# Sending the last 2 MB zero fill of GpSimd's queue as four transfers of 56, 1, 64 and 7 rows

## The chip, the cores and the metric

One core of one Trainium2 chip. The metric is device time in microseconds (us), the median over executions of the whole program. The kernel before takes 800.08 us (three runs, 799.72 to 800.21); nearly all executions here agree within 0.3%, so a few us can be told apart when runs share a chip. There are exceptions: four executions of the kernel before, on two of the chips, took 802.4 to 803.1 us, so gains of 2 to 3 us are read from several runs and with their interval.

Engines in the profile: PE is TensorE, DVE VectorE, ACT ScalarE, POOL GpSimd, SP SyncE. Transfers are issued from SyncE, ScalarE and GpSimd, and share the core's sixteen DMA engines: in the queue view below two queues fill 64.0% and 34.8% of the sixteen engines' time.

## The reference, cut to what matters

A one-token decode step (attention over the last 4,096 rows of a 32,768-row cache, then a gated layer) and its gradients for all inputs. What matters here is the size of two of the outputs: the gradients of the two caches, each 8 x 32,768 x 256 in bf16. Only the last 4,096 rows of each head carry values. The other 28,672 rows are zero, and the kernel has to write them:

```python
k = jnp.repeat(k_cache[:, :, Sk - W:, :], rep, axis=1)   # W = 4096 of Sk = 32768 rows
v = jnp.repeat(v_cache[:, :, Sk - W:, :], rep, axis=1)
...
_out, _vjp = jax.vjp(_f, A_x, A_k_cache, A_v_cache, A_wq, A_wo, B_w_gate, B_w_up, B_w_down)
_grads = _vjp(grad_out)          # d k_cache and d v_cache are zero outside the window
```

## The kernel before: the parts that matter

Nearly all of the on-chip memory (SBUF, 128 partitions side by side) is one tile, `arena`, cut by hand into column ranges. A framework (the tile layer) sees every instruction's reads and writes of a tile, orders the instructions and puts in the semaphore waits. The zero source, `zeros`, is the first ZW = 8,192 columns of that tile, of which `ar(off, n)` is the n columns from off.

```python
    TOTAL = RB + 50 * KB                          # 99,328 columns of bf16
    arena = const.tile([128, TOTAL], bf16)

    def ar(off, n):
        return arena[:, off:off + n]
    ...
    zeros = ar(0, ZW)                             # ZW = 8192: columns 0 to 8191
    ...
    s_off = RB + 38 * KB + 9 * D
    dgb = ar(s_off, 1280)
    diag = ar(s_off + 1280, 640)                  # columns 98,496 to 99,135
```

GpSimd issues 103 fills of 2 MB (128 rows of 16 KB), each reading `zeros` (13 of them its first half twice). The first 55 go out one after another in the first 344 us. The second half of `zeros` is then lent to the weight blocks, is zeroed again after the second of three blocks, and the remaining fills follow.

```python
    def send_fills(n0, n1, halves=False):
        for reg in fills[n0:n1]:
            if halves:
                ...
            else:
                ZQ.dma_start(out=reg, in_=zeros)              # line 132; ZQ is GpSimd
    ...
        for n in range(len(BLOCKS)):                          # three weight blocks
            ...
            for i in range(2):
                nc.vector.tensor_tensor(out=diag[:, 0:w]..., in0=ident_f..., in1=dgu_f...)   # line 410
                for m in range(2):
                    nc.tensor.matmul(bc_ps..., lhsT=ones_bf[:], rhs=diag...)                 # line 414
                    nc.scalar.copy(out=dgb..., in_=bc_ps...)                                 # line 415
            ...
            if n == 1:
                nc.vector.memset(ar(ZW // 2, ZW // 2), 0.0)   # line 426
                send_fills(HALF1, len(fills))
```

Nearly all of the backward pass hangs on the third block's lines 410 to 421. The last fills of all are issued from SyncE at the end, behind the results:

```python
        for o, g, n0, n1, f in late_jobs:
            reg = zero_rows(o, g, n0, n1, f)
            for i in range(reg.shape[0]):
                LD.dma_start(out=reg[i], in_=ar(2 * ZW - f, f))   # LD is SyncE
```

Of the kernel before, what the change touches and what calls it, by code (L numbers as in the profile page):

```python
# [26 lines left out]
ZW = 8192  # L27
HALF0, HALF1 = 42, 55
# [5 lines left out]
def kernel(  # L34
# [4 lines left out]
    ZQ = nc.gpsimd  # L39
# [13 lines left out]
    def ar(off, n):  # L53
        return arena[:, off:off + n]
# [4 lines left out]
    zeros = ar(0, ZW)  # L59
# [54 lines left out]
    def zero_rows(o, g, n0, n1, f):  # L114
        reg = o[0, g, 0:Sk - W, :].rearrange("s d -> (s d)")[n0 * 128 * ZW:n1 * 128 * ZW]
        return reg.rearrange("(n p f) -> n p f", p=128, f=f)

    late_jobs = [(out_2, G - 1, 5, 7, 2 * ZW), (out_3, G - 1, 0, 6, 2 * ZW), (out_3, G - 1, 6, 7, ZW)]
    fills = []
    for g in range(G):  # L120
        for o in (out_2, out_3):
            if g == G - 1 and o is out_3:
                continue
            reg = zero_rows(o, g, 0, 5 if g == G - 1 else NZ, ZW)
            fills += [reg[i] for i in range(reg.shape[0])]
# [4 lines that stand above are left out]
                ZQ.dma_start(out=reg.rearrange("p (k f) -> p k f", k=2), in_=zeros[:, 0:ZW // 2].unsqueeze(1).to_broadcast([128, 2, ZW // 2]))  # L130
            else:
                ZQ.dma_start(out=reg, in_=zeros)  # L132
# [206 lines left out]
    def block_views(n):  # L339
        f0, nb = BLOCKS[n]  # L340
        w = 128 * nb
        wgu = ar(wgu_off[n % 2], 8 * w).rearrange("p (c i f) -> p c i f", c=4, i=2)
        wd = ar(wd_off[n % 2], nb * D).rearrange("p (b n) -> p b n", n=D)
        return f0, nb, w, wgu, wd

    def load_block(n):
        f0, nb, w, wgu, wd = block_views(n)
        for eng, i, wt in ((LD, 0, B_w_gate), (nc.scalar, 1, B_w_up)):
            eng.dma_start(out=wgu[:, 0:3, i, :], in_=wt[0:384, :].rearrange("(c p) f -> p c f", c=3)[:, :, f0:f0 + w])
            eng.dma_start(out=wgu[0:DQ, 3, i, :], in_=wt[384:D, f0:f0 + w])  # L350
        LD.dma_start(out=wd, in_=B_w_down[f0:f0 + w, :].rearrange("(p b) n -> p b n", b=nb))
# [4 lines left out]
    with tc.tile_pool(name="ps_mid", bufs=3, space=bass.MemoryType.PSUM) as ps_mid, \  # L356
# [34 lines left out]
        for n in range(len(BLOCKS)):  # L391
            f0, nb, w, wgu, wd = block_views(n)
            b0 = f0 // 128
            cs = slice(b0, b0 + nb)
            for b in range(nb):
                nc.vector.tensor_tensor_reduce(out=dgb[:, 0:D], in0=wd[:, b, :], in1=dh2_bc[:], scale=1.0, scalar=0.0,
                                               op0=ALU.mult, op1=ALU.add, accum_out=d_hh[:, b0 + b:b0 + b + 1])
            gu_ps = ps_mid.tile([128, 2, 5], f32, tag="mid", name="gu_ps")
            for i in range(2):
                for b in range(nb):  # L400
                    for k in range(4):
                        kp = DQ if k == 3 else 128
                        nc.tensor.matmul(gu_ps[:, i, b:b + 1], lhsT=wgu[0:kp, k, i, b::nb], rhs=X2_b[0:kp, k:k + 1], start=(k == 0), stop=(k == 3))
            nc.vector.tensor_copy(out=gu_f[:, :, cs], in_=gu_ps[:, :, 0:nb])
            for i in range(2):
                nc.vector.tensor_tensor(out=dgu_f[:, i, cs], in0=d_hh[:, cs], in1=gu_f[:, 1 - i, cs], op=ALU.mult)
            nc.vector.tensor_tensor(out=hh_f[:, cs], in0=gu_f[:, 0, cs], in1=gu_f[:, 1, cs], op=ALU.mult)
            nc.vector.tensor_copy(out=hh_bf[:, cs], in_=hh_f[:, cs])
            for i in range(2):
                nc.vector.tensor_tensor(out=diag[:, 0:w].rearrange("p (m b) -> p m b", b=nb), in0=ident_f[:].unsqueeze(2).to_broadcast([128, 128, nb]),  # L410
                                        in1=dgu_f[:, i, cs].unsqueeze(1).to_broadcast([128, 128, nb]), op=ALU.mult)
                for m in range(2):
                    bc_ps = ps_mid.tile([128, 320], f32, tag="mid", name="bc_ps")
                    nc.tensor.matmul(bc_ps[:, 0:w // 2], lhsT=ones_bf[:], rhs=diag[:, m * w // 2:(m + 1) * w // 2], start=True, stop=True)
                    nc.scalar.copy(out=dgb[:, w * i + m * w // 2:w * i + (m + 1) * w // 2], in_=bc_ps[:, 0:w // 2])
            for b in range(nb):
                nc.tensor.matmul(ffn_ps[:], lhsT=hh_bf[:, b0 + b:b0 + b + 1], rhs=wd[:, b, :], start=(b0 + b == 0), stop=(b0 + b == NF - 1))
            for c in range(4):
                kp = DQ if c == 3 else 128
                wc = wgu[0:kp, c].rearrange("p i f -> p (i f)")  # L420
                nc.vector.tensor_tensor_reduce(out=wc, in0=wc, in1=dgb[0:kp, 0:2 * w], scale=1.0, scalar=0.0,  # L421
                                               op0=ALU.mult, op1=ALU.add, accum_out=dhn[0:kp, c, n:n + 1])
            if n + 2 < len(BLOCKS):
                load_block(n + 2)
            if n == 1:
                nc.vector.memset(ar(ZW // 2, ZW // 2), 0.0)
                send_fills(HALF1, len(fills))

        dcat2 = workm.tile([128, 8], f32)
        nc.vector.reduce_sum(out=dcat2[:, 0:4], in_=dhn[:], axis=AX)  # L430
# [57 lines left out]
    with tc.tile_pool(name="work2", bufs=2) as work2, tc.tile_pool(name="lnw", bufs=1) as lnw, \  # L488
# [164 lines left out]
        for o, g, n0, n1, f in late_jobs:  # L653
            reg = zero_rows(o, g, n0, n1, f)
# [31 lines left out]
```

## Time and profile before

| | before |
|---|---|
| median time | 800.08 us |
| span of the profiled run | 798.4 us |
| bytes moved | 334.8 MB |
| VectorE busy / TensorE busy | 51% / 59% |

The slice view of the kernel before cuts the span into 40 equal slices; a digit is a busy share in tenths, and the last row is the rate of all transfers.

```profile
DVE  2116584765846783143791579467574139573000
...
DMA  9999999999999999999999999999999999999996
GB/s 351 429 432 429 430 430 429 429 429 427 429 422 425 426 419 417 413 423 424 422 423 408 430 429 429 432 424 428 423 429 420 426 424 427 419 424 426 427 436 261
```

The DMA row is full almost everywhere: this kernel is bound by its transfers. The queue part of the page (packets, MB, share of the sixteen engines' time) shows whose they are: q0 is GpSimd's queue, q1 SyncE's.

```profile
q0 software_dynamic: 16496, 216.01, 64.0%
q1 hardware_dynamic: 11382, 116.68, 34.8%
```

The windows view of the last 16 us (busy time of each engine, then granted TensorE clock, DMA share and GB/s):

```profile
core 0: us, PE busy (x) PEld busy (x) DVE busy (x) ACT busy (x) POOL busy (x), PEclk, DMA share, GB/s
782.00:788.00 6.00, 0.00 (x0) 0.00 (x0) 0.00 (x0) 0.00 (x0) 0.00 (x0) 0.50 0.96 410
788.00:792.00 4.00, 0.00 (x0) 0.00 (x0) 0.00 (x0) 0.00 (x0) 0.00 (x0) 0.50 0.60 258
792.00:796.00 4.00, 0.00 (x0) 0.00 (x0) 0.00 (x0) 0.00 (x0) 0.00 (x0) 0.50 0.08 33
796.00:798.40 2.40, 0.00 (x0) 0.00 (x0) 0.00 (x0) 0.00 (x0) 0.00 (x0) 0.50 0.02 7
```

All engines of the core are idle and the share falls slowly: 0.08 over 4 us is little more than one DMA engine of sixteen. The trace keeps a completion record for each DMA engine of a transfer (without the engine's number). For the last store they read 789.0 us (first), 791.4 (median), 793.8 (second last) and 797.2 (last).

### The profile page before, as it was taken

How to read it: one execution, taken by the hardware profiler on the slowest of the kernel's cores; microseconds unless marked ns; L12 is line 12 of the kernel's file. 1: busy time of each engine (PE TensorE's matmuls, PEld its weight loads, DVE VectorE, ACT ScalarE, POOL GpSimd, SP SyncE). 2: the span in 40 equal slices, each digit the busy share in tenths (PEclk: the TensorE clock that was granted, in tenths of full speed). 3: DMA queues.
4: the chain of work that ended last, by engine and by line, in shares of the span. 5: the costliest groups of instructions: out<-in, count | busy, mean ns of one | idle time of the engine just before them, and what ended most of it. 6: DMA issues, size and time to landing. Idle time of an engine off the chain costs nothing.

```text
span 798.4 us, 7905 instructions
## 1 busy us (share of the span) xinstructions
PE 469.3 (59%) x3159; PEld 242.1 (30%) x3182; DVE 408.4 (51%) x728; ACT 196.2 (25%) x309; POOL 61.4 (8%) x112
## 2 busy tenths in 40 slices
PE   0459999999999998532319568565236027261000
PEld 0334545545445444311207434332103012020000
DVE  2116584765846783143791579467574139573000
ACT  0142314124132201000101127463333016242000
POOL 4000000010101111100210001000000000000000
PEclk9989999999999999555557869785558558565555
DMA  9999999999999999999999999999999999999996
GB/s 351 429 432 429 430 430 429 429 429 427 429 422 425 426 419 417 413 423 424 422 423 408 430 429 429 432 424 428 423 429 420 426 424 427 419 424 426 427 436 261
DMA packets 29354, 334.80 MB, mean 419 GB/s; under 512 B 2819, under 2 KB 5894, under 8 KB 7814
## 3 DMA queue, kind: packets, MB, share of 16 engines
q0 software_dynamic: 16496, 216.01, 64.0%
q1 hardware_dynamic: 11382, 116.68, 34.8%
q10 hardware_dynamic: 1440, 1.61, 0.6%
q8 instruction: 25, 0.41, 0.2%
q14 instruction: 11, 0.09, 0.0%
HBM read 53.69 MB, written 280.59 MB: 419 GB/s over the span
## 4 chain that ended last, share of the span: by engine, by line
PE 40%; DMA 28%; DVE 15%; ACT 4%; issue 2%; another core or an unknown queue 0%; SPq 0%; ACTq 0%; DVEq 0%
DMA out_dram<-arena 18%; PE M_ps L309 13%; PE ok_ps L313 8%; PE rows_ps L255 7%; PE tr_ps L252 5%; DMA dh_bc<-in_grad_out_dram 4%; ACT arena L269 3%; DVE arena L643 2%; DVE arena L644 2%; DMA arena<-in_A_wo_dram 2%; DVE arena L452 2%; PE dqb_ps L495 2%; DMA arena<-in_B_w_up_dram 2%; DMA arena<-in_B_w_gate_dram 2%; DVE arena L421 2%
## 5 line engine op out<-in xcount | busy, mean ns | idle before, releaser
L304 DVE TENSOR_TENSOR arena<-arena,p_f 128x2048 bf16<-128x2048 bf16 x64 | 145.2, 2284 | 58.7 <-PE M_ps L309 58.7
L309 PE MATMUL M_ps<-arena 128*128 128x512 bf16 x489 | 126.4, 381 | 1.1
L255 PE MATMUL rows_ps<-arena,vpad 128*16 128x512 bf16 x256 | 85.6, 430 | 23.1 <-DVE arena L606 17.1
L252 PE MATMUL tr_ps<-ident_bf,arena 128*128 128x128 bf16 x1024 | 87.8, 236 | 14.2 <-DMA arena<-in_A_k_cache_dram 7.2
L132 POOL DMA_DIRECT2D out_dram<-arena x90 | 48.2, 537 | 549.4 <-DMA out_dram<-arena 495.6
L252 PEld LDWEIGHTS <-arena 128*128 128x128 bf16 x1024 | 66.0, 105 | 63.5 <-issue 55.6
L636 PE MATMUL d_ps<-arena,rT 32*128 32x512 bf16 x256 | 44.6, 508 | 67.1 <-DVE arena L644 49.1
L269 ACT COPY arena<-tr_ps 128x1024 bf16<-128x1024 bf16 x64 | 61.7, 1015 | 69.3 <-PE tr_ps L252 69.3
L313 PE MATMUL ok_ps<-arena 128*16 128x256 bf16 x512 | 64.6, 273 | 1.1 <-DVE arena L296 0.9
L309 PEld LDWEIGHTS <-arena 128*128 128x128 bf16 x512 | 43.3, 99 | 51.0 <-issue 15.3
L604 ACT COPY arena<-tr_ps 128x1024 bf16<-128x1024 bf16 x32 | 32.5, 1017 | 95.7 <-PE tr_ps L252 39.1
L640 ACT CAST arena<-d_ps 128x512 bf16<-128x512 f32 x64 | 37.7, 589 | 72.4 <-PE d_ps L636 72.4
L643 DVE CAST arena<-d_ps 128x512 bf16<-128x512 f32 x64 | 43.9, 686 | 14.2 <-PE d_ps L636 14.0
L313 PEld LDWEIGHTS <-arena 128*16 128x16 bf16 x512 | 41.9, 89 | 29.9 <-issue 21.0
L644 DVE CAST arena<-d_ps 128x512 bf16<-128x512 f32 x64 | 43.5, 679 | 7.6 <-DMA out_dram<-arena 7.6
L636 PEld LDWEIGHTS <-rT 32*128 32x128 bf16 x256 | 11.5, 95 | 93.9 <-issue 51.1
L641 ACT CAST arena<-d_ps 128x512 bf16<-128x512 f32 x64 | 38.1, 595 | 7.5 <-DMA out_dram<-arena 7.5
L255 PEld LDWEIGHTS <-vpad 128*16 128x16 bf16 x256 | 19.3, 91 | 57.0 <-issue 49.3
L507 DVE CUSTOM_DVE_ANT_0 arena<-arena 128x4096 bf16<-128x4096 bf16 x3 | 13.1, 4422 | 24.4 <-ACT arena L500 24.4
L284 ACT ACTIVATE e_f<-cols_ps,nbias 128x32 f32<-128x32 f32 x16 | 4.5, 286 | 85.7 <-DVE nbias L280 85.7
L257 DVE COPY arena<-rows_ps 16x512 f32<-16x512 f32 x16 | 10.8, 675 | 28.7 <-PE rows_ps L255 28.7
L606 DVE COPY arena<-tr_ps 128x1024 bf16<-128x1024 bf16 x32 | 21.7, 680 | 3.5 <-PE tr_ps L252 3.4
(198 smaller groups left out, 373.8 us busy)
## 6 DMA issues: line engine op xcount, KB each, us to landing
out_dram<-arena POOLq DMA_DIRECT2D x103, 2048.0 KB, 52.6
out_dram<-arena SPq DMA_DIRECT2D x18, 2048.0 KB, 33.8
arena<-in_A_v_cache_dram SPq DMA_DIRECT2D x10, 2048.0 KB, 49.4
arena<-in_A_k_cache_dram SPq DMA_DIRECT2D x8, 2048.0 KB, 28.6
out_dram<-arena SPq DMA_DIRECT2D x4, 4096.0 KB, 46.1
arena<-in_A_wq_dram SPq DMA_DIRECT2D x2, 3072.0 KB, 20.4
arena<-in_A_wo_dram SPq DMA_DIRECT2D x2, 1792.0 KB, 16.2
out_dram<-arena SPq DMA_DIRECT2D x2, 1792.0 KB, 32.9
```

The costliest lines, as they stand in the source:

```text
L132: ZQ.dma_start(out=reg, in_=zeros)
L252: nc.tensor.transpose(tr_ps[:, dh, i, :], X_sb[:, 4 * q + i, dh * 128:(dh + 1) * 128], ident_bf[:])
L255: nc.tensor.matmul(rows_ps[:], lhsT=pad[:, dh, 16 * q:16 * q + 16], rhs=XT[:, dh].rearrange("p t k -> p (t k)"), start=(q == 0 and dh == 0 ...
L269: sT_ps = dots(kv_at(K_off[g]), KT_slot, vpad[g % 2], rows1, ps_c, "cols", lambda q, XT, ps: nc.scalar.copy(out=XT, in_=ps))
L304: nc.vector.tensor_tensor(out=pK, in0=K_sb[:, 4 * c:4 * c + 4, :].unsqueeze(2).to_broadcast([128, 4, 2, Dh]), in1=p_f[:, c::8, :].unsqueez ...
L309: nc.tensor.matmul(M_ps[:, vh, :], lhsT=V_sb[:, t, vh * 128:(vh + 1) * 128], rhs=pK[:, i, :, :].rearrange("p h d -> p (h d)"), start=(t == ...
L313: nc.tensor.matmul(ok_ps[:, k, :], lhsT=ppad[g % 2][:, 8 * (t % 4) + t // 4, :], rhs=X_sb[:, t, :], start=(g == 0 and k == 0 and t == 0), ...
L636: nc.tensor.matmul(d_ps[:, qi].rearrange("p w d -> p (w d)"), lhsT=rT[32 * q:32 * (q + 1), :], rhs=RB_[32 * q:32 * (q + 1), l, :], start=T ...
L640: nc.scalar.copy(out=stV[:, t:t + 2, :], in_=d_ps[:, :, 0, :])
L641: nc.scalar.copy(out=stK[:, t:t + 2, :], in_=d_ps[:, :, 1, :])
L643: nc.vector.tensor_copy(out=stV[:, t:t + 2, :], in_=d_ps[:, :, 0, :])
L644: nc.vector.tensor_copy(out=stK[:, t:t + 2, :], in_=d_ps[:, :, 1, :])
```

## The change

Intent: one DMA engine of sixteen ends the kernel alone. By a premise of the prediction (its source is given there), a transfer from GpSimd whose outermost size is k below sixteen goes on k engines. So the last fill is cut in such a way that one engine (number 7, if the count starts at 0) gets one row, its seven other rows going to engines 0 to 6. To keep every engine reading from its own place in SBUF, the source rows are taken from every fourth partition, and each is read repeatedly.

```diff
             if n == 1:
                 nc.vector.memset(ar(ZW // 2, ZW // 2), 0.0)
-                send_fills(HALF1, len(fills))
+                send_fills(HALF1, len(fills) - 1)
+                reg = fills[-1]
+                for p0, step, r0, k, m in ((0, 4, 0, 7, 8), (28, 4, 127, 1, 1), (64, 4, 56, 8, 8), (0, 4, 120, 7, 1)):
+                    ZQ.dma_start(out=reg[r0:r0 + k * m].rearrange("(k m) f -> k m f", m=m),
+                                 in_=zeros[p0:p0 + step * (k - 1) + 1:step].unsqueeze(1).to_broadcast([k, m, ZW]))
```

## The prediction

> **What bounds the kernel now.** Transfers. In the slice view the DMA row is at nine tenths in 39 of 40 slices; the DMA part gives 334.8 MB at a mean of 419 GB/s over 798.4 us. PE is busy 59%, DVE 51%, and the timeline shows no compute after 734 us. The change writes the same 2 MB, so only the balance of the sixteen DMA engines can move.
>
> That balance is not perfect. In the windows view the DMA share is 0.97 in 780 to 788 us, 0.77 in 788 to 790, 0.44, then 0.10 in 792 to 794 and 0.06 in 794 to 796 (25 GB/s): one engine of sixteen works alone at the end. The completion records of the last store agree: its engines report at 789.0 (first), 791.4 (median), 793.8 (second last) and 797.2 us (last). GpSimd's last fill: 731.1 first, 736.8 second last, 741.5 last; on most earlier fills the last report is 2 to 10 us behind the second. It looks like one fixed slow engine. The Trainium skill, "DMA: Bandwidth & Descriptors", section "Latency and other measured facts", says that engines 7 and 15 are usually slower; the trace carries no engine number, so it cannot say which.
>
> **What the change does.** The same page, section "Why a DMA increments its semaphore by 16 and not by 1", says that a GpSimd transfer whose outermost size is k below 16 goes on k consecutive engines from a round-robin cursor. If the cursor stands at 0, the 56 rows are engines 0 to 6 with eight rows each, the single row is engine 7, the 64 rows are engines 8 to 15 with eight each, and the last seven rows go to 0 to 6. Engine 7 does one row instead of eight, engines 0 to 6 nine.
>
> **Cost.** In the tail, a store of eight 16 KB rows per engine takes about 4.9 us (spacing of successive stores' reports), so a row is 0.62 us. Seven rows off: 4.3 us. If engine 7 is the straggler, it ends at 797.2 - 4.3 = 792.9; engines 0 to 6 end 0.6 later than now; the second-slowest then ends last, at 793.8 (794.4 if it is one of 0 to 6). Gain 2.8 to 3.4 us, all on the critical path, since the stream on that engine is unbroken to the end.
>
> Added: three more GpSimd issues of about 0.53 us (timeline of POOL). Each waits for the landing of an earlier fill: I expect issues at about 688, 692, 702 and 712 us, ahead of 725 to 731 us, where their bytes come up. That costs nothing.
>
> **Prediction.** 797.0 us, range 796.2 to 800.6; chances: faster by over 2% 0.01, within 2% 0.98, slower by over 2% 0.01. About 65% for a gain of some 3 us, 20% for none (the slow engine is another), 15% for a cursor elsewhere (0 to 0.6 us slower, or more if shares pile up on a few engines).
>
> **What would show it.** Right: the last store's second-last and last reports under 1.5 us apart, a steeper fall of the DMA share at the end, same bytes, issues at the times above. Wrong: the straggler still alone for 3 us and a span of 798 or 799. If the clusters pile up on the same engines, half of the engines end some 5 us early.
>
> **What would make it wrong.** The cursor does not start at 0, or keeps its place between executions (it advances by 23, so by 7 modulo 16), which would spread repeated runs; the straggler is another engine; or a transfer with k below 16 is spread differently.

## More of the kernel before

GpSimd's fills are filler for stretches in which SyncE has nothing ready.

VectorE at the third block's line 410 (the timeline: start, duration, instruction), for comparison later. It follows line 406 with one copy between them and no idle time:

```profile
384.55 0.21 DVE L406 TENSOR_TENSOR dgu_f<-d_hh,gu_f 128x5 f32<-128x5 f32 x2
384.69 0.67 DVE L606 COPY arena<-tr_ps 128x1024 bf16<-128x1024 bf16 x1
385.29 0.80 DVE L410 TENSOR_TENSOR arena<-ident_f,dgu_f 128x640 bf16<-128x640 f32 x1
```

The stretch from there to the end, as a window:

```profile
core 0: us, PE busy (x) PEld busy (x) DVE busy (x) ACT busy (x) POOL busy (x), PEclk, DMA share, GB/s
...
385.29:798.40 413.11, 170.62 (x1125) 89.53 (x1124) 208.56 (x466) 112.39 (x183) 22.09 (x41) 0.64 0.99 417
```

and how long SyncE's 2 MB stores take from issue to landing (median, the last number):

```profile
out_dram<-arena SPq DMA_DIRECT2D x18, 2048.0 KB, 33.8
```

## The result, and the profile after

| | before | after |
|---|---|---|
| median time | 800.03 us (4 runs) | 930.75 us (4 runs, 929.72 to 931.56) |
| span of the profiled run | 798.4 us | 927.9 us |
| bytes moved | 334.80 MB | 334.80 MB |
| mean rate | 419 GB/s | 361 GB/s |

The ratio is 1.1634 (95% interval 1.1614 to 1.1654). Ratios here are the mean time of one kernel's fast runs over that of the other's of the same rounds, so not quite the ratio of the medians in the table. The same bytes took 130 us longer.

The slice view after, the same rows as shown before:

```profile
DVE  2038556755768214400000000007538889979820
...
DMA  9999999999999999999999999970350446797978
GB/s 360 429 431 429 429 429 429 429 427 427 428 420 421 411 420 424 424 426 426 422 422 423 421 424 423 422 324 0 159 182 0 170 185 271 327 409 304 422 319 384
```

VectorE is idle in slices 18 to 27 while transfers run at full rate; after that, compute runs and the transfers have holes, two slices of them at 0 GB/s. The waits view after (who waited for whom: total us, times, longest) names the place:

```profile
ACT arena L608 <- DMA out_dram<-arena: 264.1, 1, 264.1
...
PE bc_ps L414 <- DVE arena L410: 246.9, 4, 243.6
DVE arena L410 <- DMA out_dram<-arena: 241.5, 1, 241.5
```

One single wait of 241.5 us of VectorE at line 410, and one of 264.1 us of ScalarE at line 608 (the copy of a transposed tile into `arena`, the first of the second phase), both for fills to land. TensorE then waits for VectorE. In the timeline of VectorE, in place of the three lines shown of before:

```profile
384.45 0.22 DVE L406 TENSOR_TENSOR dgu_f<-d_hh,gu_f 128x5 f32<-128x5 f32 x2
626.16 0.83 DVE L410 TENSOR_TENSOR arena<-ident_f,dgu_f 128x640 bf16<-128x640 f32 x1 [241.49 <-DMA out_dram<-arena]
```

The four new transfers themselves were issued from GpSimd, 2 to 5 us apart, 87 to 99 us earlier than the last fill of the kernel before (688 us), and they landed by 626.0 us:

```profile
581.00 0.53 POOL L132 DMA_DIRECT2D out_dram<-arena  x1 [4.49 <-DMA out_dram<-arena]
588.74 0.60 POOL L430 DMA_DIRECT2D out_dram<-arena  x1 [7.20 <-issue]
590.93 0.50 POOL L430 DMA_DIRECT2D out_dram<-arena  x1 [1.59 <-DMA out_dram<-arena]
596.05 0.58 POOL L430 DMA_DIRECT2D out_dram<-arena  x1 [4.62 <-DMA out_dram<-arena]
601.05 0.51 POOL L430 DMA_DIRECT2D out_dram<-arena  x1 [4.42 <-DMA out_dram<-arena]
```

So while VectorE waited, GpSimd's queue had the DMA engines to itself (99.8 MB of its fills moved in 385 to 626 us, and nothing of SyncE's) and ran dry. The windows view, cut at the end of the wait:

```profile
core 0: us, PE busy (x) PEld busy (x) DVE busy (x) ACT busy (x) POOL busy (x), PEclk, DMA share, GB/s
384.50:626.16 241.66, 0.00 (x0) 0.00 (x0) 0.17 (x4) 0.00 (x0) 23.75 (x45) 0.50 0.98 414
626.16:927.90 301.74, 165.90 (x1125) 87.14 (x1125) 208.33 (x466) 112.85 (x184) 0.00 (x0) 0.71 0.58 241
```

Now the loss can be placed (this is bookkeeping; the cause is tested below). The second phase, from line 410 to the end, has the same compute in both (VectorE 208.3 and 208.6 us busy). It takes 413.1 us before and 301.7 after: 111.4 us shorter. It moved about 172 MB before (413.1 us at 417 GB/s) and 73 MB after, because the fills were done by then, and SyncE's stores no longer share the engines with them:

```profile
out_dram<-arena SPq DMA_DIRECT2D x18, 2048.0 KB, 10.7
```

(33.8 us to landing before, 10.7 now.) The wait moved the start of that phase from 385.3 to 626.2, by 240.9 us. 240.9 - 111.4 = 129.5 us, the difference of the two spans. Seen from the transfers: the 72.7 MB left after the wait (301.74 us at 241 GB/s) would have taken 174 us at the 417 GB/s of before; they took 128 us more, nearly the whole loss.

The programs as built say the same. Listed here are all waits of compute engines on the completion counts of GpSimd's last fills. The kernel before has none; after has six, on three of the four new transfers:

```
new transfer   source access pattern (partition step, count), ...   completion count
56 rows        [397312, 7] [0, 8] [1, 8192]                         A
1 row          [397312, 1] [512, 16] [1, 512]                       B
64 rows        [397312, 8] [0, 8] [1, 8192]                         C
7 rows         [397312, 7] [1, 8192]                                D

VectorE, before line 410 : waits for A, C, D
ScalarE, before line 608 : waits for A, C, D
```

A partition is 99,328 elements away from the next, so 397,312 is a step of four partitions. The three that are waited for are the three with such a step; the transfer of one row has a count of 1 there and is waited for by nobody. The repeated reading (step 0, count 8) is not the trigger: the 7 rows have none and are waited for. Line 410 writes columns 98,496 to 99,135 of `arena`, the fills read columns 0 to 8,191. Nothing overlaps: the wait protects nothing.

### The profile page after: what moved, and what is told of

Same layout as the page of the kernel before. It is cut to its first block, busy times and chain, and to the rows that moved or that the text cites. A ratio compares the mean times of both kernels' runs of the same rounds, so it can differ in the third digit from the quotient of the medians.

```text
span 927.9 us, 7912 instructions
## 1 busy us (share of the span) xinstructions
PE 464.4 (50%) x3159; PEld 239.6 (26%) x3182; DVE 407.7 (44%) x728; ACT 195.6 (21%) x309; POOL 62.8 (7%) x115
## 2 busy tenths in 40 slices
DMA packets 29563, 334.80 MB, mean 361 GB/s; under 512 B 3013, under 2 KB 6104, under 8 KB 8024
## 4 chain that ended last, share of the span: by engine, by line
DMA 50%; DVE 16%; another core or an unknown queue 13%; PE 10%; issue 3%; ACT 2%; POOL 1%; DVEq 0%; ACTq 0%; POOLq 0%
DMA out_dram<-arena 50%; PE rows_ps L255 3%; DVE arena L647 3%; DVE arena L648 3%; DVE arena L536 2%; DVE arena L456 2%; PE dqb_ps L499 2%; PE d_ps L640 2%; PE tr_ps L252 1%; DVE arena L633 1%; POOL out_dram L132 1%; DVE arena L511 1%; DVE arena L610 1%; DVE arena L421 1%
## 5 line engine op out<-in xcount | busy, mean ns | idle before, releaser
L414 PE MATMUL bc_ps<-arena,ones_bf 128*128 128x320 bf16 (+1 forms) x12 | 4.0, 439 | 246.9 <-DVE arena L410 246.9
L410 DVE TENSOR_TENSOR arena<-ident_f,dgu_f 128x640 bf16<-128x640 f32 (+1 forms) x6 | 4.7, 780 | 243.1 <-DMA out_dram<-arena 241.5
L608 ACT COPY arena<-tr_ps 128x1024 bf16<-128x1024 bf16 x32 | 32.6, 1018 | 337.3 <-DMA out_dram<-arena 264.1
## 6 DMA issues: line engine op xcount, KB each, us to landing
out_dram<-arena SPq DMA_DIRECT2D x18, 2048.0 KB, 10.7
```

## The experiments

**Theory A**: the source's partition step of 4 makes the dependency tracking treat the read as touching far more of `arena` than it does; the next writes of VectorE and ScalarE into `arena` are made to wait for the last fills; that wait, and nothing else, costs the 130 us. **Theory B**: transfers confined to seven and eight DMA engines are what is slow.

### e1: the step of 4, on all sixteen engines

```diff
-                for p0, step, r0, k, m in (...):
-                    ZQ.dma_start(...)
+                ZQ.dma_start(out=reg.rearrange("(k m) f -> k m f", m=8),
+                             in_=zeros[0:61:4].unsqueeze(1).to_broadcast([16, 8, ZW]))
```

> The last fill as ONE transfer on all sixteen engines, eight rows each, but read from every fourth partition (0, 4, ... 60). Theory A (the partition step of 4 makes the program's dependency tracking treat the read as touching far more of the arena than it does, so later writes of VectorE and ScalarE into the arena are made to wait for the last fills): as slow as the change, 920 to 935 us, with VectorE at line 410 idle some 240 us until an out_dram<-arena transfer lands. Theory B (transfers on seven and eight engines are what costs): about 800 us and no such wait.

Measured: 934.02 us, ratio 1.1681 (1.1663 to 1.1698). The waits view of e1 (ScalarE's line is numbered 607 here):

```profile
ACT arena L607 <- DMA out_dram<-arena: 268.6, 1, 268.6
...
DVE arena L410 <- DMA out_dram<-arena: 245.6, 1, 245.6
```

No uneven transfer is left, and the loss is whole. Theory B cannot explain this run.

### e2: the uneven transfers, without the step

```diff
-                                 in_=zeros[p0:p0 + step * (k - 1) + 1:step].unsqueeze(1)...
+                                 in_=zeros[p0:p0 + k].unsqueeze(1)...
```

> The same four transfers on seven, one, eight and seven engines, but read from neighbouring partitions (step 1). Theory A: the wait at line 410 is gone and the time is back at 795 to 806 us (a few us more than aimed at if neighbouring partitions are read more slowly). Theory B: still about 930 us.

Measured: 813.88 us, ratio 1.0177 (1.0161 to 1.0193). The wait is gone: VectorE's idle time ahead of line 410 is 3.0 us, all of it for TensorE, as in the kernel before (the source view of line 410):

```profile
its engine sat idle before it (us, times) until:
  PE bc_ps L414: 3.0, 3
```

That is theory A's main forecast. The time lies above the band I gave it (795 to 806), and the windows view shows where: the rate while these transfers run, e2 first, the kernel before second.

```profile
core 0: us, PE busy (x) PEld busy (x) DVE busy (x) ACT busy (x) POOL busy (x), PEclk, DMA share, GB/s
724.00:740.00 16.00, 1.11 (x8) 0.11 (x4) 2.58 (x4) 2.15 (x4) 0.00 (x0) 0.50 1.05 243
```

```profile
core 0: us, PE busy (x) PEld busy (x) DVE busy (x) ACT busy (x) POOL busy (x), PEclk, DMA share, GB/s
724.00:740.00 16.00, 1.23 (x8) 0.22 (x8) 3.01 (x5) 2.42 (x5) 0.00 (x0) 0.50 1.03 427
```

The cause fits the Trainium skill, "SBUF — State Buffer", section "Door 1: The DMA port swizzle": four neighbouring partitions share one of sixteen ports, so seven engines that read partitions 0 to 6 pull through two ports. The trace agrees as far as it goes (243 against 427 GB/s in the same 16 us); no run measured a port by itself. The step of 4 was thus there for a reason.

### e3: a real wait, first try

```diff
                 send_fills(HALF1, len(fills))
+                nc.vector.memset(ar(0, 2), 0.0)
```

> The kernel before, with one tiny VectorE memset of two columns of the zero source put behind the last fills, a genuine hazard: it must wait until all fills have been read. Theory A says that the cost is that wait alone, so a kernel whose transfers are all unchanged gets as slow as the change: 915 to 935 us, with VectorE idle some 240 us. Theory B: about 800 us, as no transfer has been changed.

Measured: 800.28 us, ratio 1.0005 (0.9989 to 1.0022): no loss. The timeline of VectorE shows why this says nothing against theory A:

```profile
737.35 0.06 DVE L428 MEMSET arena<- 128x1 uint32 x1 [16.04 <-DMA out_dram<-arena]
```

The framework ordered the memset, on which nothing depends, behind all of VectorE's work; it waited there for the fills, at no cost. The place of a line in the source is not its place on the engine. The run was inconclusive and the experiment was made again as e8.

### e8: a real wait, on the path

```diff
+                diag = ar(0, 640) if n == 2 else ar(s_off + 1280, 640)   # third block: inside the zero source
                 nc.vector.tensor_tensor(out=diag[:, 0:w]...
 ...
+        nc.vector.memset(ar(0, 640), 0.0)                                # zero it again
```

> The kernel before with all its transfers unchanged, but VectorE's line 410 of the third weight block writes its 640 columns into the zero source itself (and zeroes them again afterwards): a genuine hazard, which VectorE cannot put off as it did in e3, since the forward and backward chain hangs on it. Theory A (the cost of the change is that wait alone): 925 to 940 us with VectorE idle some 240 us at line 410. Theory B: about 800 us.

Measured: 929.92 us, ratio 1.1622 (1.1606 to 1.1638), correct. The waits view of e8 (line 410 is 411 here):

```profile
DVE arena L411 <- DMA out_dram<-arena: 240.6, 1, 240.6
```

All transfers are those of the kernel before. One wait of 240.6 us at that one line is enough to make 800 us into 930. The change measured 930.75.

### e4 and e11: the four transfers and the step, but the zero source in its own tile

```diff
-    arena = const.tile([128, TOTAL], bf16)
+    zero_part = const.tile([128, ZW], bf16)
+    arena = const.tile([128, TOTAL - ZW], bf16)
     def ar(off, n):
+        if off < ZW: return zero_part[:, off:off + n]
-        return arena[:, off:off + n]
+        return arena[:, off - ZW:off - ZW + n]
 ...                                              # SyncE's late fills read zero_part twice
-                LD.dma_start(out=reg[i], in_=ar(2 * ZW - f, f))
+                LD.dma_start(out=reg[i].rearrange("p (k f) -> p k f", f=ZW), in_=zeros.unsqueeze(1).to_broadcast([128, f // ZW, ZW]))
```

(The memset for the second half of the old source falls away.) e11 is the same with the last fill plain.

> The changed kernel with its four transfers and the step of 4 left as they are, but the 16 KB zero source made a tile of its own beside the rest of the arena, so that no later write shares a tile with the read (the last fills of SyncE's queue then read that source twice instead of a 32 KB row). Theory A: no wait at line 410; 796 to 801 us; if engine 7 is the straggler, some 3 us under the kernel before and the last two reports of the last store within 1.5 us. Theory B: about 930 us.

> Control for e4: the zero source as a tile of its own and the last SyncE fills read twice from it, but the last GpSimd fill plain. If e4's 1.5 us over the kernel before came with the split, this is 801 to 802; if from the four transfers, 800.

Measured: e4 801.46 us, ratio 1.0022 (1.0007 to 1.0037); e11 800.55 us, ratio 0.9999 (0.998 to 1.0018), on another chip. In e4 VectorE's idle time ahead of line 410 (414 there; 414 has become 418) is again 3.0 us, for TensorE:

```profile
its engine sat idle before it (us, times) until:
  PE bc_ps L418: 3.0, 3
```

The change is intact, step included, and the 130 us are gone. e11, with no loss, lays e4's 1.5 us to the four transfers and not to the split, as far as runs on two chips can. With e1, e2 and e8 this settles theory A: what triggers the wait is a partition step in a source that shares its tile with later writes.

But the gain of 3 us has not appeared either. That part of the prediction had to be tried by itself.

### e5, e6, e7: the intended balance, with no wait in the way

The four transfers are written after the last compute, where no write of `arena` follows. e6 is the control: the plain fill moved to that place. In e7 the sizes are 64, 56, 1 and 7 rows.

```diff
-                (the four transfers at n == 1)
 ...
+        reg = fills[-1]
+        for p0, step, r0, k, m in ((0, 4, 0, 7, 8), (28, 4, 127, 1, 1), (64, 4, 56, 8, 8), (0, 4, 120, 7, 1)):
+            ZQ.dma_start(...)                    # as in the change
         for o, g, n0, n1, f in late_jobs:
```

> The four transfers exactly as in the change, but written after the last compute instead of before the third weight block, so that no arena write follows them and none can be made to wait. Theory A: no wait at line 410. If in addition the balance argument holds (cursor at 0, engine 7 the straggler): 796 to 798 us, 2.5 to 4 us under e6, and the last store's last two reports within 1.5 us. If the straggler is another engine: within 1 us of e6. If the cursor is elsewhere: 0 to 1 us over e6, with a spread among repeated runs.

> Control for e5: the kernel before, with its last fill (one plain transfer of 128 rows) moved to the same late place. 799.5 to 801 us by every theory; the last engine reports the last store about 3 us behind the second last, as before.

> As e5, but the sizes arranged so that with a cursor at 0 engine 15, not engine 7, gets one row instead of eight (64 rows on eight engines, 56 on seven, 1, 7). If engine 7 is the straggler: no gain over e6 (0 to +1 us). If engine 15 is it: 2.5 to 4 us under e6, and e5 shows no gain. If neither gains, the straggler is a third engine or the cursor is not at 0.

| | median us | last store: first report | second last | last |
|---|---|---|---|---|
| before | 800.01 (9 runs) | 789.0 | 793.8 | 797.2 |
| e6, plain fill, late | 800.07 | 791.2 | 796.8 | 797.9 |
| e5, 56/1/64/7 | 800.76 | 788.8 | 794.9 | 797.7 |
| e7, 64/56/1/7 | 800.88 | 784.5 | 793.8 | 797.9 |

(Report times are those of each profiled run; that of before is its own first profile.) No gain in either: ratios 1.0009 (0.9996 to 1.0023) and 1.0010 (0.9998 to 1.0023). In e7 one engine ends 4.0 us ahead of the next: an engine has been relieved, but not the one that ends the kernel.

Two reasons are in the traces. First, the single row did not go on one engine. The packets of GpSimd's queue after the change include sixteen of 1,024 bytes, which the kernel before has none of: the row of 8,192 elements was cut into sixteen pieces of 512, as its access pattern above already shows. It ran on all sixteen: in e5 the sixteen packets start between 725.6 and 741.5 us, each 0.5 to 0.7 us before one of the sixteen reports of that transfer. So it did not give one engine a single row. Second, the engine that ends last did eight rows within the first transfer in both runs: its report of the first transfer lies 6.1 us behind its report of the fill before (735.7 to 741.8 in e5, 735.5 to 741.6 in e7). It is among the first seven from the cursor, not behind them.

### e9: which pair?

The last fill, in e5's place, as eight transfers of two engines with eight rows each.

```diff
+        for p0, step, k, m in ((0, 4, 2, 8), (8, 4, 2, 8), (16, 4, 2, 8), (24, 4, 2, 8), (64, 4, 2, 8), (72, 4, 2, 8), (80, 4, 2, 8), (88, 4, 2, 8)):
```

> A look, not an improvement: in e5's late place the last fill goes as eight transfers of two engines each, eight rows per engine, so every engine does as much as before, but each pair in its own transfer. An engine's report of a transfer comes late by its eight rows only in its own pair's transfer. The engine that ends the kernel should jump by 5 to 9 us in exactly one of the eight; which one tells its place from the cursor. From e5 and e7, where that engine did eight rows in the first transfer (seven and eight engines), I expect one of the first four pairs. If the cursor were not used at all (all transfers on the lowest engines), the last reports would run away by tens of us.

Measured: 800.22 us in one look. The last reports of the eight transfers are at 736.7, 738.0, 743.6, 751.0, 757.1, 762.1, 767.0 and 771.9 us, behind 735.5 for the fill before. My forecast of exactly one jump failed: from the third on every step is 5 to 7 us. From about 743.8 on this engine is busy with SyncE's stores at full rate (it reports one of 4 MB, sixteen rows of 16 KB to an engine, 9.7 us behind the store before it, at 753.5 and 743.8), so that the later reports only queue behind those. Its own eight rows, about 4.9 us of work, must then lie before 743.8, and the steps to 736.7 and 738.0 are too short for them. That leaves the third pair, engines 4 and 5 from the cursor: an inference, tested in e15. (The runaway by tens of us that would mean an unused cursor did not come: the last store ended at 797.3, as before.)

### e10: one engine relieved without a single-row transfer

```diff
+        for p0, step, k, m in ((0, 4, 8, 1), (64, 4, 8, 8), (0, 4, 7, 8)):
```

> What the change set out to do, with no single-row transfer: packets of 1 KB in the trace say that the single row was cut into sixteen pieces over all engines[...]. Here 8 rows go to eight engines (one each), 64 to the next eight and 56 to the next seven: with a cursor at 0 engine 7 gets one row, engines 0 to 6 nine. If engine 7 is the straggler: 1 to 3.5 us under e6 (796.5 to 799). If it is one of the first seven from the cursor, as e5 and e7 suggest: 0 to 1 us over e6, and one engine reports some 4 us early.

Measured: 808.56 us, ratio 1.0096 (1.0079 to 1.0113), outside every case I had written down. One engine reports the last store 4.6 us ahead of the next (788.2 and 792.8), so someone was relieved, but two others end at 805.1 and 806.5. The windows view of e10 shows 304 GB/s where the kernel before has 427:

```profile
core 0: us, PE busy (x) PEld busy (x) DVE busy (x) ACT busy (x) POOL busy (x), PEclk, DMA share, GB/s
724.00:740.00 16.00, 0.61 (x4) 0.11 (x4) 1.60 (x3) 1.21 (x3) 0.00 (x0) 0.50 1.03 304
```

e7, with nearly the same pieces in another order, has 425 there. The recut transfers of e10 seem to have got in each other's or SyncE's way. A possible reading is that its first transfer, with no repetition of a row, was dealt out in another way than I assumed, so that the later ones read from other engines' partitions. No run tests that; it stays open.

### e12 and e13: the same question on SyncE's queue

The Trainium skill, "DMA: Bandwidth & Descriptors", section "Why a DMA increments its semaphore by 16 and not by 1", says that a SyncE transfer with k below 16 uses the lowest-numbered k engines. No cursor is involved. Only SyncE's very last 2 MB fill is recut.

```diff
+        LD.dma_start(out=reg[0:86].rearrange("r f -> (r f)").rearrange("(p w) -> p w", p=128), in_=zeros[:, 0:5504])
+        LD.dma_start(out=reg[86:128].rearrange("(k m) f -> k m f", m=6),
+                     in_=zeros[0:25:4].unsqueeze(1).to_broadcast([7, 6, ZW]))        # e12; e13: 88 rows, then 8 x 5
```

> Which engine ends the kernel, asked without GpSimd's cursor. The kernel before, with only SyncE's very last 2 MB fill recut: 86 rows evenly on all sixteen engines (5.4 rows each) and 42 rows as one transfer on seven engines (six rows each). The Trainium skill says that a SyncE transfer with k below 16 takes the lowest-numbered engines: engines 0 to 6 then do 11.4 rows (2.1 us more than now), 7 to 15 do 5.4 (1.6 us less). If the straggler is 7 (or 15): about 798.4 us, 1.6 under the kernel before. If it is one of 0 to 6: about 802, 2 over.

> As e12, but 88 rows evenly (5.5 each) and 40 on eight engines (five each): engines 0 to 7 do 10.5 rows (1.5 us more), 8 to 15 do 5.5 (1.5 us less). If the straggler is 7: about 801.6 us where e12 gains. If it is 15: about 798.5, as e12. If it is one of 0 to 6: both e12 and e13 lose 1.5 to 2 us.

Measured: e12 802.13 us, ratio 1.0026 (1.0012 to 1.004); e13 801.49 us, ratio 1.0018 (1.0006 to 1.0031). Against the medians of before on that chip (800.03) that is 2.1 and 1.5 us more, the two figures forecast for a straggler among engines 0 to 6. The records bear it out: the part transfer (the one on seven or eight engines) has seven landings in e12 and eight in e13, each with one more update soon after the issue, and in e12 the last landing of the seven engines is at 798.9, which is the straggler's report of the part before, 795.3, plus six rows (3.7 us) within 0.1 us.

So, on that statement of the skill, the engine that ends this kernel is one of 0 to 6. The change set out to relieve number 7. In e12 and e13 the low-numbered half is also slower as a whole: in e13, its eight engines land the part transfer at 792.1 to 798.7. Less their five further rows (3.1 us) that is 789.0 to 795.6, which fits the eight latest reports of the even part, 789.1 to 795.7; the eight earliest, then those of the other engines, end at 788.7.

### e14 and e15: the same tool, aimed at the right half

In e5's place, two transfers in e14 and four in e15:

```diff
+        for p0, step, k, m in ((0, 4, 8, 3), (64, 4, 8, 13)):                            # e14
+        for p0, step, k, m in ((0, 4, 4, 6), (16, 4, 2, 2), (24, 4, 2, 6), (64, 4, 8, 11)):   # e15
```

> The last GpSimd fill in e5's late place as two transfers of eight engines: three rows each on the first eight from the cursor, thirteen on the next eight (five rows, 3.1 us, moved from each of the first to each of the second). e12 and e13 put the straggler in engines 0 to 6 and show that all of 0 to 7 end later than nearly all of 8 to 15. With the cursor at 0: straggler 797.9 - 3.1, second half up by 3.1 to about 793.5: 796.8 to 798.2 us, some 2 to 3 us under the control e6 and under the kernel before. With the cursor at 8: 802 to 804.

> As e14, with four transfers: six rows on each of the first four engines, two on the next two, six on the next two, eleven on the last eight. If the straggler is engine 4 or 5, as e9 suggests: it gives up 3.7 us, the other low engines 1.2, the high ones take on 1.8: 796 to 797.3 us. If it is another of 0 to 7: only 1.2 us under e6, about 799.

Measured: e14 797.36 us, ratio 0.9973 (0.996 to 0.9987); e15 797.41 us, ratio 0.9969 (0.9957 to 0.9982); before 800.05 on the same chip. Both are 0.3% under the kernel before: little, and "the same" by a bar of 2%, but their intervals leave out 1. e6, the plain fill in this place, gained nothing. The windows view of e14's end:

```profile
core 0: us, PE busy (x) PEld busy (x) DVE busy (x) ACT busy (x) POOL busy (x), PEclk, DMA share, GB/s
782.00:788.00 6.00, 0.00 (x0) 0.00 (x0) 0.00 (x0) 0.00 (x0) 0.00 (x0) 0.50 0.95 410
788.00:792.00 4.00, 0.00 (x0) 0.00 (x0) 0.00 (x0) 0.00 (x0) 0.00 (x0) 0.50 0.84 356
792.00:795.80 3.80, 0.00 (x0) 0.00 (x0) 0.00 (x0) 0.00 (x0) 0.00 (x0) 0.50 0.11 47
```

The share falls later and more steeply than in the kernel before (0.84 where that had 0.60, for 788 to 792 us), and the last store's last two reports are at 794.3 and 794.6, 0.3 us apart, where the kernel before had 3.4. Thus the tool works once it is aimed at the half with the late engine, which is the first eight from the cursor, as a cursor at 0 would have it. The reverse cut (thirteen rows on the first eight) was not run. e15's profiled run, at 796.29 us, has its last report at 793.4; if the straggler had been another of the first eight I had it at 799. That supports engines 4 and 5, and e15's completion records settle the pair: the late engine reports the fill before at 735.0 and the four transfers at 736.0, 737.6, 738.6 and 739.7. No step has room for six rows (3.7 us) or eleven (6.8 us); the second, of 1.6, fits two rows (1.2 us), and those were given to the fifth and sixth engine from the cursor. But e15's five runs spread from 796.29 to 799.12 (of e14's, four lie between 797.09 and 797.52 and one at 799.95), and its median is no better than e14's, so the finer aim has not been shown to be worth anything.

## Why the prediction was wrong

- **Bound by transfers, one engine ends alone**: right. Bytes did not change, and e14 shows that balance is worth 2.7 us.
- **"Added: three more GpSimd issues [...] That costs nothing."** This is the step that failed, and it alone is the 130 us. I counted what the new transfers cost GpSimd and the DMA engines, and did not ask which instructions would have to wait for them. They read a tile that VectorE and ScalarE go on writing, and they read it with a partition step, which no fill did before. The wait of 241.5 us at line 410 came of it (e1, e4: with the step and without; e8: the wait alone). Its price is not its length: 111 us came back because the fills were done during the wait, and 130 us did not, because 72.7 MB were left for a phase that, without filler, kept the DMA engines busy for a share of 0.58 only.
- **The issue times** (688, 692, 702 and 712 us) were wrong as a consequence: 589 to 601 us were measured, as SyncE sent nothing while the wait lasted.
- **The straggler as engine 7**: wrong. I took it from the skill, which has 7 and 15 as usually slower, and gave it 65%. e12 and e13 put it in 0 to 6, by the lowest-numbered rule that they rest on; e15 makes it the fifth or sixth from GpSimd's cursor.
- **One row on one engine**: wrong. It was cut into sixteen pieces. Even without the wait, the change gains nothing (e5: 0.7 us over its control).
- **0.62 us per row, 3 us in all**: about right as a size. e14 moved five rows, 3.1 us by that figure, off the late half and gained 2.7.
- The range (796.2 to 800.6) and the chance of 0.01 for slower by over 2% took the framework's waits for granted. The listed ways to be wrong were all about the DMA engines.

Left open: what inside the tracking turns a partition step into a wait (only what triggers it is shown); e10's loss of rate; why one low-numbered engine is late, and whether it is the same one on every chip (e5, e9, e12 and e15 ran on four); where GpSimd's cursor stands, which no record shows; the spread of e15 and the one slower run of e14.

## What to carry to other kernels

A transfer's cost includes the waits that it hangs on others. When a new access reads a tile that is written later, compare the waits of the built program before and after, engine by engine; an access pattern of a new kind (here a partition step) on a tile shared by many unrelated ranges is enough for a wait that protects nothing, and a tile of its own, or a place behind the last write, removes it. In a kernel that is full of background transfers, a stall lets the background run dry, and the foreground pays for it later. Before moving work off a slow DMA engine, find out which one it is with a run made for that.

## What the Trainium skill lacked or had wrong

- "DMA: Bandwidth & Descriptors", section "Latency and other measured facts", says that engines 7 and 15 are usually slower. Here the engine that ends last is another, one of 0 to 6: moving 2.1 us of rows onto them cost 2.1 us (e12), 1.5 us onto 0 to 7 cost 1.5 us (e13), while relieving 0 to 7 gained 2.7 us (e14). The number rests on the same page's lowest-numbered rule.
- The same page, section "Why a DMA increments its semaphore by 16 and not by 1", counts engines by the slowest dimension that is not of size 1 and says that software can split a contiguous row; the prediction overlooked this when it put one row on one engine. What the section does not say is that a single row cut from a larger pattern is split unasked: 16 packets of 1,024 bytes here.
- The same section's rules on which engines are used (lowest-numbered for SyncE, from a cursor for GpSimd) are only partly borne out: seven landings for k = 7 and eight for k = 8 fit its count, and e14 and e15 fit a cursor at 0, but no run shows an engine's number, and e10 did not come out as its cursor would have it.
- No page says that a partition step in a transfer's source can make later writes elsewhere in the same tile wait: 241.5 us here.

Neither lacking nor wrong: "SBUF — State Buffer", section "Door 1: The DMA port swizzle", agrees with e2 (243 GB/s with neighbouring source partitions, 427 before).
